# Block transposes on VectorE, 32-row score tiles and a pipeline two batches deep in a longformer-and-mixer kernel

## The chip, the cores and the metric

The kernel runs on one core of one Trainium2 chip. The metric is the device time of one execution in microseconds (us), lower is better. The profiled span, from the first to the last instruction, is 1.7 to 2.0 us shorter than the time of the same run. Positions in time below are us from the start of that span.

## The reference

The input is `q`, `k`, `v` of shape 8 x 8 x 576 x 64 (batch, head, position, depth) and eight sorted `global_idx`. A banded attention with eight global positions feeds an MLP-mixer block:

```python
scores = scale * q @ k.T                                   # per batch and head, 576 x 576
mask = (abs(i - j) <= 32) | is_global[i] | is_global[j]
attn = softmax(where(mask, scores, -1e9))
x = (attn @ v) with heads side by side                     # 8 x 576 x 512
u = x + transpose(relu(x.T @ w_tok1) @ w_tok2)             # w_tok1: 576 x 256
out = u + relu(u @ w_ch1) @ w_ch2                          # w_ch1: 512 x 1536, float32 out
```

(Shortened from numpy; the normalisation of the softmax is as usual.)

## The kernel before

Each batch is a run of units. The names are those that the profile shows:

- `T` turns q and k of a head pair from rows by position into columns (tile `pT`). `S_` makes the banded scores of a pair (`s`), with eight columns for the global queries, then `exp` (`e_all`), the band mask, and `eg`, the weights of the global queries.
- `GK` (`gk`) makes the scores of every query against the eight global keys. `OG` (`og`) sums the outputs of the global queries over all keys: the global sums.
- `PV` (`pv`) is the banded attention output, normalised into `x`. `M1` (`a1p`) and `M2` (`hp`) mix tokens, `M3` (`pu`) transposes, and `M4` (`b1p`) and `M5` (`op`) mix channels. An odd batch carries the last 64 positions of two batches as an extra tail.

```python
def cast(b, t=None):            # cut
    nc.scalar.copy(out=s["qn"][:, sl], in_=n32[0][:, sl])
    nc.vector.tensor_copy(out=s["kn"][:, sl], in_=n32[1][:, sl])
    nc.gpsimd.tensor_copy(out=vsh[b % 2][:, sl, :, 0:D], in_=n32[2][:, sl])

def T(b, p):
    pT = pss([P, 2, 8 * P], F16, name=f"pT_{b}_{p}")
    for ti, n in enumerate(("qn", "kn")):
        for t in range(NT):
            nc.tensor.transpose(out=pT[:, ti, P * t : P * t + P],
                                in_=s[n][:, t, 2 * p : 2 * p + 2, :], identity=ident)
    # ... GpSimd: global columns of qT, zero margin of kT; VectorE: two copies out of PSUM

def S_(b, p):                   # cut: score(ps, off, c) is, for the two heads of the pair,
    nc.tensor.matmul(ps[:, par, off : off + n], lhsT=kT[r, P * c : P * c + P],
                     rhs=qf[r, lo : lo + n], start=True, stop=True)   # r: 64 rows
    # ... ScalarE: exp into e_all; VectorE: mask; GpSimd: eg

def OG(b):
    for c in range(NT):
        for hf in range(2):
            nc.tensor.matmul(ps[:, hf, 0 : 4 * VW], lhsT=eg[:, c],
                rhs=vsh[b % 2][:, c, 4 * hf : 4 * hf + 4, :], start=(c == 0), stop=(c == NT - 1))
    # ... VectorE: the wanted blocks into rf, plus vg (the gathered v rows)

# the main loop: all attention and token mixing of batch b+1 between the M4 and M5 of batch b
for b in range(B):
    if b + 1 < B:
        cast(b + 1)
        globals_(b + 1)
    if b + 2 < B:
        load(b + 2)
    merge(sparse(b + 1) if b + 1 < B else [], dense(b))
```

The order of the emitted instructions is a hint only: a scheduler may reorder them on each engine.

The softmax here doesn't subtract the row's maximum and nothing guards it: scores larger than these inputs give would overflow.

Of the kernel before, what the change touches and what calls it, by code (L numbers as in the profile page):

```python
# [14 lines left out]

P = 128
# [6 lines left out]


def merge(sparse, dense):

    ts, td = sum(c for c, _ in sparse) or 1.0, sum(c for c, _ in dense) or 1.0
    i = j = 0
    a = d = 0.0
    while i < len(sparse) or j < len(dense):  # L30
        if j >= len(dense) or (i < len(sparse) and a / ts <= d / td):
            a += sparse[i][0]
            sparse[i][1]()
            i += 1
        else:
            d += dense[j][0]
            dense[j][1]()
            j += 1
# [3 lines left out]
def kernel(  # L42
# [18 lines left out]
    NP = H // 2  # L61
    NJ = DCH // P
    assert S == 576 and D == 64 and DM == 512 and DTOK == 256 and DCH == 1536
    LAST = S - P * (NT - 1)

    const = ctx.enter_context(tc.tile_pool(name="const", bufs=1))
    ab = ctx.enter_context(tc.tile_pool(name="ab", bufs=2))
    pb = ctx.enter_context(tc.tile_pool(name="pb", bufs=6))
# [15 lines left out]


    n32 = [const.tile([P, NT, H, D], F32, name=f"n32_{n}") for n in "qkv"]
    nc.gpsimd.memset(n32[0][LAST:P, NT - 1], 0.0)
    nc.gpsimd.memset(n32[1][LAST:P, NT - 1], 0.0)
    nc.gpsimd.memset(n32[2][0:WIN, 0], 0.0)
    nc.gpsimd.memset(n32[2][P - WIN : P, NT - 1], 0.0)  # L90

    def load(b):
        for ti, ten in enumerate((q, k)):
            for t in range(NT):
                n = P if t < NT - 1 else LAST
                nc.sync.dma_start(
                    out=n32[ti][0:n, t], in_=ten[b, :, P * t : P * t + n, :].rearrange("h p d -> p h d")
                )
        for c in range(NT):
            r0 = WIN if c == 0 else 0  # L100
            r1 = P - WIN if c == NT - 1 else P
            j0 = P * c - WIN + r0
            nc.sync.dma_start(
                out=n32[2][r0:r1, c], in_=v[b, :, j0 : j0 + (r1 - r0), :].rearrange("h p d -> p h d")
            )

    load(0)


    gt32 = global_idx.tensor.bitcast(I32)  # L110
    gidx_b = const.tile([P, NG], I32)
    nc.scalar.dma_start(out=gidx_b, in_=bass.AP(tensor=gt32, offset=0, ap=[[0, P], [2, NG]]))
    gidx_f = const.tile([P, NG], F32)
    nc.vector.tensor_copy(out=gidx_f, in_=gidx_b)

    ident = const.tile([P, P], F16)
    make_identity(nc, ident)
    pi_i = const.tile([P, 1], I32)
    nc.gpsimd.iota(pi_i, pattern=[[1, 1]], base=0, channel_multiplier=1)

    def int_op(name, in_, s, op):
        t = const.tile([P, 1], I32, name=name)
        nc.vector.tensor_scalar(out=t, in0=in_, scalar1=s, scalar2=None, op0=op)
        return t

    def to_f(name, in_):
        t = const.tile([P, 1], F32, name=name)
        nc.vector.tensor_copy(out=t, in_=in_)
        return t

    pf = to_f("pf", pi_i)
    p8 = to_f("p8", int_op("p8i", pi_i, 3, ALU.logical_shift_right))
    p16 = to_f("p16", int_op("p16i", pi_i, 4, ALU.logical_shift_right))
    pm8 = to_f("pm8", int_op("pm8i", pi_i, 7, ALU.bitwise_and))
    pm16 = to_f("pm16", int_op("pm16i", pi_i, 15, ALU.bitwise_and))

    it_i = const.tile([P, NT * P], I32)
    nc.gpsimd.iota(it_i, pattern=[[1, NT * P]], base=0, channel_multiplier=0)
    it_f = const.tile([P, NT * P], F32)
    nc.vector.tensor_copy(out=it_f, in_=it_i)  # L140


    oh = const.tile([P, NG], F32)
    gpp = const.tile([P, 1], F32)
    nc.vector.tensor_scalar(out=oh, in0=it_f[:, 0:NG], scalar1=pm8, scalar2=None, op0=ALU.is_equal)
    nc.vector.tensor_mul(out=oh, in0=oh, in1=gidx_f)
    nc.vector.reduce_sum(out=gpp, in_=oh, axis=AX.X)


    idx_i = const.tile([P, 4 + B], I32)  # L150
    base2 = const.tile([P, 1], F32)
    nc.vector.tensor_scalar(out=base2, in0=p8, scalar1=float(2 * S), scalar2=gpp, op0=ALU.mult, op1=ALU.add)
    for t in range(2):
        for par in range(2):
            nc.vector.tensor_scalar(
                out=idx_i[:, 2 * t + par : 2 * t + par + 1], in0=base2,
                scalar1=float((32 * t + par) * S), scalar2=None, op0=ALU.add,
            )
    basev = const.tile([P, 1], F32)
    nc.vector.tensor_scalar(out=basev, in0=p16, scalar1=float(S), scalar2=gpp, op0=ALU.mult, op1=ALU.add)  # L160
    for b in range(B):
        nc.vector.tensor_scalar(
            out=idx_i[:, 4 + b : 5 + b], in0=basev, scalar1=float(b * H * S), scalar2=None, op0=ALU.add
        )


    d1 = const.tile([P, H], F32)
    d2 = const.tile([P, H], F32)
    lo8 = const.tile([P, 1], F32)
    hi8 = const.tile([P, 1], F32)  # L170
    nc.vector.tensor_scalar(out=lo8, in0=pm16, scalar1=7.5, scalar2=None, op0=ALU.is_lt)
    nc.vector.tensor_scalar(out=hi8, in0=pm16, scalar1=7.5, scalar2=None, op0=ALU.is_gt)
    nc.vector.tensor_scalar(out=d1, in0=it_f[:, 0:H], scalar1=p16, scalar2=lo8, op0=ALU.is_equal, op1=ALU.mult)
    nc.vector.tensor_scalar(out=d2, in0=it_f[:, 0:H], scalar1=p16, scalar2=hi8, op0=ALU.is_equal, op1=ALU.mult)


    mf = const.tile([P, NT * P], F16)
    onm = const.tile([P, NT * P], F16)
    nc.vector.tensor_scalar(out=mf, in0=it_f, scalar1=gpp, scalar2=lo8, op0=ALU.is_equal, op1=ALU.mult)
    nc.vector.tensor_scalar(out=onm, in0=it_f, scalar1=float(S) - 0.5, scalar2=hi8, op0=ALU.is_lt, op1=ALU.mult)  # L180
    nc.vector.tensor_add(out=mf, in0=mf, in1=onm)


    colng = const.tile([P, NT * P], F16)
    colt = const.tile([P, NT * P], F16)
    nc.vector.tensor_scalar(out=colng, in0=it_f, scalar1=float(S) - 0.5, scalar2=None, op0=ALU.is_lt)
    for g in range(NG):
        nc.vector.tensor_scalar(out=colt, in0=it_f, scalar1=gidx_f[:, g : g + 1], scalar2=None, op0=ALU.not_equal)
        nc.vector.tensor_mul(out=colng, in0=colng, in1=colt)
    bandm = const.tile([P, NT, EW - 64], F16)  # L190
    nc.gpsimd.memset(bandm, 1.0)
    rowok = const.tile([P, NT], F32)
    dk = const.tile([P, NG], F32)
    for c in range(NT):
        nc.vector.tensor_scalar(
            out=dk, in0=gidx_f, scalar1=pf, scalar2=float(-(P * c - WIN)), op0=ALU.subtract, op1=ALU.add
        )
        nc.vector.tensor_mul(out=dk, in0=dk, in1=dk)
        nc.vector.tensor_scalar(out=dk, in0=dk, scalar1=0.5, scalar2=None, op0=ALU.is_gt)
        rk = rowok[:, c : c + 1]  # L200
        nc.vector.tensor_reduce(out=rk, in_=dk, axis=AX.X, op=ALU.min)
        if c == 0:
            nc.vector.memset(rowok[0:WIN, 0:1], 0.0)
        if c == NT - 1:
            nc.vector.memset(rowok[P - WIN : P, c : c + 1], 0.0)

        left, right = bandm[:, c, 0:64], bandm[:, c, 72:200]
        nc.gpsimd.affine_select(out=left, in_=left, compare_op=ALU.is_ge, fill=0.0, base=0, pattern=[[1, 64]], channel_multiplier=-1)
        nc.gpsimd.affine_select(out=right, in_=right, compare_op=ALU.is_ge, fill=0.0, base=64, pattern=[[1, P]], channel_multiplier=-1)
        nc.gpsimd.affine_select(out=right, in_=right, compare_op=ALU.is_ge, fill=0.0, base=0, pattern=[[-1, P]], channel_multiplier=1)  # L210
        nc.vector.tensor_scalar_mul(out=bandm[:, c, :], in0=bandm[:, c, :], scalar1=rk)
        if c > 0:
            nc.vector.tensor_mul(out=left, in0=left, in1=colng[:, P * c - 64 : P * c])
        else:
            nc.vector.memset(left, 0.0)
        nc.vector.tensor_mul(out=right, in0=right, in1=colng[:, P * c : P * c + P])


    e_all = const.tile([P, H, NT, EW], F16)
    nc.vector.memset(e_all, 0.0)  # L220
    eg = const.tile([P, NT, H, 16], F16)
    nc.gpsimd.memset(eg, 0.0)
    kgz = [const.tile([P, NP, 32], F16, name=f"kgz{i}") for i in range(2)]
# [59 lines left out]


    st = [dict() for _ in range(B)]

    def cast(b, t=None):
        s = st[b]
        if "qn" not in s:
# [259 lines left out]
    for t in range(NT):  # L549
        cast(0, t)  # L550
# [43 lines left out]
```

## Time and profile before

| | before |
|---|---|
| median of 3 runs (range) | 426.28 us (424.61 to 428.53) |
| profiled span | 422.7 us |
| first `M4` matmul of batch 0 | 94.7 us |
| first `M4` to first `M4`, batches 0 to 6 | 43.0, 45.4, 40.4, 45.4, 40.4, 43.8, 38.4 us |
| from the first `M4` of batch 7 to the end | 31.2 us |

The last three rows come from the timeline of TensorE: find the first matmul into `b1p` of each batch and subtract. Their sum is the span, which makes a ledger in which any change must show up.

From the page of the kernel before, the busy times and four rows of the 40 slices (each digit is the busy share of a slice of 10.6 us, in tenths; PEclk is the granted TensorE clock in tenths):

```profile
...
PE 331.2 (78%) x2756; PEld 179.0 (42%) x2756; DVE 212.5 (50%) x434; ACT 150.0 (35%) x273; POOL 94.2 (22%) x197
...
PE   0120242678799979997999799979998999899995
...
POOL 9578842020410032003120311031201000100000
PEclk9999999999699999999999999999999999999999
...
```

TensorE's digit is at most 2 in each of the first five slices, while that of GpSimd (POOL) is 5 to 9. From the tenth slice to the last but one it runs at 70 to 99%, and about every fourth slice is at 7 or 8.

The view of chosen stretches gives, for each, its length, the busy time of each engine with the number of instructions, the clock, the share of the DMA engines and GB/s:

```profile
...
core 0: us, PE busy (x) PEld busy (x) DVE busy (x) ACT busy (x) POOL busy (x), PEclk, DMA share, GB/s
0.00:50.00 50.00, 5.23 (x28) 2.27 (x30) 25.39 (x111) 6.69 (x7) 39.86 (x78) 1.00 1.02 164
...
183.00:201.00 18.00, 14.60 (x129) 7.27 (x127) 10.90 (x19) 14.63 (x28) 4.24 (x14) 1.00 0.49 90
201.00:223.70 22.70, 22.70 (x195) 12.77 (x194) 12.80 (x22) 2.81 (x4) 3.36 (x2) 1.00 0.60 133
...
183.10:268.90 85.80, 79.22 (x691) 43.22 (x689) 47.32 (x83) 36.49 (x67) 15.44 (x32) 1.00 0.53 111
...
```

There are two sorts of steady stretch. In 201 to 223.7 us TensorE is busy the whole time. In 183 to 201 us it works 14.60 of 18.00 us, and ScalarE, with 14.63 us, is just as loaded. The last line is a pair of batches, an even and an odd one: TensorE is busy 79.22 of 85.80 us, so 6.6 us of a pair are idle, or 3.3 us per batch.

The list of TensorE's waits up to the first `M4` (who waited, for whom, us in total, times, longest):

```profile
...
PE s_0_0_405 L336 <- POOL kT_0_383 L321: 16.1, 1, 16.1
PE og_528 L382 <- POOL eg L358: 10.9, 1, 10.9
...
```

The first score matmul waits 16.1 us for a small GpSimd memset that stands behind gathers and weight loads in GpSimd's order. The first `OG` waits 10.9 us for `eg`, on the same engine. (The largest total of the list, 16.9 us in five waits, is that of the first transposes for the cast of q, which itself waits for its load.)

TensorE's timeline at the end of a half-loaded stretch (start, duration, what, count, and the wait before it in brackets):

```profile
...
196.79 0.32 PE L369 MATMUL gk_1957<-qT_0_1781,kgz_252 128*32 128x384 f16 x1 [0.35 <-ACT e_all L345]
...
198.26 1.02 PE L492 MATMUL b1p_8_1991<-uT_1716,wc_274 128*128 128x512 f16 x4 [1.00 <-ACT b_2_1787 L495]
199.88 1.30 PE L382 MATMUL og_1976<-vsh_256,eg 128*128 128x264 f16 x10 [0.60 <-POOL eg L358]
```

Score, `exp`, mask, `eg`, `OG` is one chain inside one batch. ScalarE serves the score `exp`s and the `Relu`s of `M4` together, so TensorE waits now for `e_all`, now for `b`, now for `eg`.

### The profile page before, as it was taken

The page shows a single profiled execution, that of the slowest core. Times are in us where ns is not written, and L with a number is a line of the kernel's source. Part 1 is how long each engine was busy: PE and PEld are TensorE (multiplying, and loading weights), DVE is VectorE, ACT ScalarE, POOL GpSimd, SP SyncE. Part 2 cuts the span into 40 slices and gives each one's busy share as a digit, 9 for nine tenths or more (in the row PEclk, how much of TensorE's full clock was granted, in tenths as well). Part 3 has the DMA queues.
Part 4 walks back from the last instruction along what each step waited for, and adds up shares of the span by engine and source line. Part 5 has one row for each costly group of instructions (what it writes and reads, how often), then busy time and mean ns, then how long its engine had stood idle before and what let it go on. Part 6 is the DMA issues. An engine that isn't in the chain of part 4 may idle for free.

```text
span 422.7 us, 6930 instructions
## 1 busy us (share of the span) xinstructions
PE 331.2 (78%) x2756; PEld 179.0 (42%) x2756; DVE 212.5 (50%) x434; ACT 150.0 (35%) x273; POOL 94.2 (22%) x197
## 2 busy tenths in 40 slices
PE   0120242678799979997999799979998999899995
PEld 0000121444365437453645374536454745364452
DVE  4792070484545555466555653574555535556111
ACT  1202150218510772049106820392057203810520
POOL 9578842020410032003120311031201000100000
PEclk9999999999699999999999999999999999999999
DMA  1999999996927094616660847100110021001012
GB/s 25 191 207 198 205 198 215 206 189 118 187 54 173 26 170 80 163 50 124 128 161 28 140 86 186 51 0 2 51 50 3 2 76 50 2 26 50 25 47 79
DMA packets 123472, 42.48 MB, mean 101 GB/s; under 512 B 114609, under 2 KB 118577, under 8 KB 123441
## 3 DMA queue, kind: packets, MB, share of 16 engines
q1 hardware_dynamic: 112512, 28.32, 37.2%
q10 hardware_dynamic: 6288, 9.44, 6.5%
q0 software_dynamic: 4640, 4.29, 6.0%
q8 instruction: 21, 0.34, 0.3%
q14 instruction: 11, 0.08, 0.1%
HBM read 36.38 MB, written 9.44 MB: 108 GB/s over the span
## 4 chain that ended last, share of the span: by engine, by line
PE 58%; ACT 11%; DVE 11%; DMA 9%; POOL 5%; issue 4%; POOLq 0%; DVEq 0%; ACTq 0%
ACT e_all L345 4%; DVE e_all L357 3%; DMA gidx_b<-in_global_idx_dram 3%; DMA n_v<-in_v_dram 3%; ACT e_all L354 2%; ACT e_all L353 2%; DMA w_271<-in_moe_w_tok_dram 1%; DMA g_k_281<-in_k_dram,idx_i 1%; ACT e_all L352 1%; POOL eg L358 1%; DVE x_0_257 L424 1%; POOL vsh_255 L295 1%; DMA n_k<-in_k_dram 1%; PE op_4_4516 L518 1%; PE op_4_3805 L518 1%
## 5 line engine op out<-in xcount | busy, mean ns | idle before, releaser
L357 DVE TENSOR_TENSOR e_all<-e_all,bandm 128x1000 f16<-128x1000 f16 x64 | 40.8, 678 | 53.3 <-ACT e_all L354 49.9
L492 PEld LDWEIGHTS <-wc_274 128*128 128x128 f16 x384 | 34.4, 98 | 45.4 <-issue 16.2
L358 POOL COPY eg<-e_all 128x80 f16<-128x80 f16 x32 | 10.5, 327 | 81.7 <-DVE e_all L357 80.9
L412 PEld LDWEIGHTS <-e_all 128*128 128x128 f16 x320 | 24.9, 100 | 3.0 <-issue 1.7
L417 PEld LDWEIGHTS <-e_all 128*128 128x128 f16 x256 | 19.1, 101 | 1.3
L382 PEld LDWEIGHTS <-eg 128*128 128x128 f16 x80 | 8.1, 109 | 21.3 <-POOL eg L358 19.5
L295 POOL CAST vsh_256<-n_v 128x2560 f16<-128x2560 f32 x4 | 9.3, 2316 | 29.9 <-PE pv_4_1063 L412 8.6
L295 POOL CAST vsh_255<-n_v 128x512 f16<-128x512 f32 (+1 forms) x8 | 9.8, 1263 | 24.4 <-DMA n_v<-in_v_dram 9.3
L315 PE MATMUL pT_0_371<-ident,qn_322 128*128 128x128 f16 x5 | 1.4, 289 | 16.9 <-ACT qn_322 L293 16.9
L336 PE MATMUL s_0_0_405<-qT_0_382,kT_0_383 64*128 64x200 f16 x4 | 0.5, 351 | 16.1 <-POOL kT_0_383 L321 16.1
L454 PEld LDWEIGHTS <-w_273 128*128 128x128 f16 x80 | 7.8, 97 | 12.0 <-issue 3.2
L505 PEld LDWEIGHTS <-wc_274 128*128 128x128 f16 x192 | 11.1, 98 | 0.9
L382 PE MATMUL og_528<-vsh_255,eg 128*128 128x264 f16 x10 | 2.4, 425 | 10.9 <-POOL eg L358 10.9
L315 PEld LDWEIGHTS <-qn_322 128*128 128x128 f16 x20 | 1.9, 127 | 18.7 <-ACT qn_322 L293 17.7
L436 PEld LDWEIGHTS <-w_271 128*128 128x128 f16 x64 | 6.3, 99 | 7.3 <-issue 1.1
L293 ACT CAST qn_697<-n_q 128x2560 f16<-128x2560 f32 x1 | 2.3, 2324 | 18.9 <-DMA n_q<-in_q_dram 18.9
L522 DVE TENSOR_TENSOR osb_0_4465<-u_7_4235,op_0_4452 128x512 f32<-128x512 f16 x1 | 0.7, 686 | 15.1 <-PE op_0_4452 L518 15.1
L336 PEld LDWEIGHTS <-kT_0_383 64*128 64x128 f16 x10 | 0.7, 129 | 17.1 <-issue 16.1
L293 ACT CAST qn_322<-n_q 128x512 f16<-128x512 f32 x5 | 3.1, 617 | 12.7 <-DMA n_q<-in_q_dram 12.7
L315 PE MATMUL pT_0_371<-ident,kn_323 128*128 128x128 f16 x5 | 1.4, 288 | 7.4 <-DVE kn_323 L294 7.4
L518 PEld LDWEIGHTS <-b_7_4324 128*128 128x128 f16 x48 | 4.7, 98 | 5.4
L293 ACT CAST qn_1189<-n_q 128x2560 f16<-128x2560 f32 x1 | 2.3, 2325 | 12.8 <-DMA n_q<-in_q_dram 12.8
(1293 smaller groups left out, 957.5 us busy)
## 6 DMA issues: line engine op xcount, KB each, us to landing
n_q<-in_q_dram SPq DMA_DIRECT2D x32, 256.0 KB, 5.1
n_k<-in_k_dram SPq DMA_DIRECT2D x32, 256.0 KB, 5.3
n_v<-in_v_dram SPq DMA_DIRECT2D x24, 256.0 KB, 5.4
n_v<-in_v_dram SPq DMA_DIRECT2D x16, 192.0 KB, 5.0
wc_274<-in_moe_w_ch_dram POOLq DMA_DIRECT2D x3, 512.0 KB, 10.3
wc_275<-in_moe_w_ch_dram POOLq DMA_DIRECT2D x3, 512.0 KB, 17.3
n_q<-in_q_dram SPq DMA_DIRECT2D x8, 128.0 KB, 4.9
n_k<-in_k_dram SPq DMA_DIRECT2D x8, 128.0 KB, 4.8
```

The source lines that it names most:

```text
L295: nc.gpsimd.tensor_copy(out=vsh[b % 2][:, sl, :, 0:D], in_=n32[2][:, sl])
L345: nc.scalar.activation(out=e2[:, :, 1:3, 64:EW], in_=s1[:, :, 0:400].rearrange("p h (c x) -> p h c x", c=2), func=AF.Exp, scale=scale)
L353: nc.scalar.activation(out=e2[:, :, 4, 64 : 64 + QS], in_=s2[:, :, 136:272], func=AF.Exp, scale=scale)
L354: nc.scalar.activation(out=e2[:, :, 3, 64:EW], in_=s2[:, :, 272:472], func=AF.Exp, scale=scale)
L357: nc.vector.tensor_mul(out=eh, in0=eh, in1=bandm)
L358: nc.gpsimd.tensor_copy(out=eg[:, :, 2 * p : 2 * p + 2, 0:NG], in_=e2[:, :, :, P:QS].rearrange("p h c x -> p c h x"))
L382: nc.tensor.matmul(ps[:, hf, 0 : 4 * VW], lhsT=eg[:, c], rhs=vsh[b % 2][:, c, 4 * hf : 4 * hf + 4, :], start=(c == 0), stop=(c == NT - 1),)
L412: nc.tensor.matmul(o, lhsT=e_all[:, h, tau, QS - sh : QS - sh + P], rhs=vsh[b % 2][:, tau, h, :], start=False, stop=last and tau == NT - 1,)
L417: nc.tensor.matmul(o, lhsT=e_all[:, h, tau + 1, 0:P], rhs=vsh[b % 2][:, tau + 1, h, :], start=False, stop=last)
L492: nc.tensor.matmul(ps, lhsT=wc1[:, cc, P * j : P * j + P], rhs=s["uT"][:, cc, :], start=(cc == 0), stop=(cc == 3))
L505: nc.tensor.matmul(ps[:, i, :], lhsT=wc1[:, cc, P * j : P * j + P], rhs=s["uTl"][:, cc, :], start=(cc == 0), stop=(cc == 3),)
L518: nc.tensor.matmul(ps, lhsT=w, rhs=wc2[:, j, :], start=(j == 0), stop=(j == NJ - 1))
```

## The change

The intent is to take work off TensorE and ScalarE in the steady state and to shorten the prologue.

- q and k are loaded as float16 by casting DMAs (only batch 0's q is still cast on ScalarE), with positions spread so that VectorE can turn them: a 32 x 32 block transpose on pairs of float16 seen as one int32. TensorE's 40 transposes per batch, the two casts and the PSUM copies go.
- A pair of depth elements now shares an int32, so a score needs two accumulating matmuls with 32 rows in place of one with 64. Four heads stand in the four row groups. `GK` is tiled by rows and columns.
- `OG` is tiled by columns: four groups of 32 columns, two heads each, with half the streamed width. One-hot rows in `eg` let it pick the global v rows as well, which makes the eight v gathers unnecessary.
- The schedule is the program order on every engine. One half of a batch merges `OG`, `PV` and `M1` of batch b+1 and the VectorE transposes of b+2 into `M4` of b. The other half merges `M2` and `M3` of b+1 and the scores of b+2 into `M5` of b.
- A new prologue gathers for batches 0 to 3 only before use, and finishes the scores of batch 1 before the dense work of batch 0 begins.

```diff
+    ctx.enter_context(tc.manual_schedule(engines=ORDERED))          # ORDERED = None
...
-        for ti, n in enumerate(("qn", "kn")):
-            for t in range(NT):
-                nc.tensor.transpose(
...
+    def Xk(b, hg):
+        nc.vector.transpose(
+            out=kTs[b % 2][:, hg, WIN : WIN + S].rearrange("p (i r) -> p r i", r=RK),
+            in_=st[b]["k16"].bitcast(I32)[:, hg].rearrange("p (r j) -> p r j", r=RK),
+        )
...
+            for e in range(2):
+                for r in range(4):
+                    rs = slice(32 * r, 32 * r + 32)
+                    nc.tensor.matmul(
+                        tiles[r // 2][:, r % 2, off : off + n], lhsT=kT[rs, P * c : P * c + P, e],
+                        rhs=qf[rs, lo : lo + n, e], start=(e == 0), stop=(e == 1),
+                    )
...
+            for r in range(4):                                       # OG
                 nc.tensor.matmul(
-                    ps[:, hf, 0 : 4 * VW], lhsT=eg[:, c],
-                    rhs=vsh[b % 2][:, c, 4 * hf : 4 * hf + 4, :], start=(c == 0), stop=(c == NT - 1),
+                    ps[32 * r : 32 * r + 32, 0, 0 : 2 * VW].rearrange("p (g x) -> p g x", g=2), lhsT=egs[b % 2][:, c, r],
+                    rhs=vsh[b % 2][:, c, r::4, :], start=(c == 0), stop=(c == NT - 1),
                 )
...
+    globals_k(0)                                                     # prologue, cut
+    flush()
+    vcast(0)
+    # (two memsets) load_v(1), load_k(1, 1), load_q(1, 1)
+    u_S(0, 1, 0)()
+    u_S(0, 1, 1)()
+    u_GK(0, psv)()
+    flush()
+    # (wc1 and wc2 loads, OG and PV and M1 of batch 0, transposes of batch 1)
+    sp = phase_m(0)
+    for i, (_, f) in enumerate(phase_s(1)):
+        if i < len(sp):
+            run(sp[i][1])
+        run(f)
+    flush()
+    vcast(1)
+    gather(gq, q, 1)                                                 # gathers of batches 4 to 7
+    gather(gk, k, 1)
+    gather_t(gq, gqT, 1)
+    gather_t(gk, gkT, 1)
+    load_qk(2)
+    load_v(2)
+    for b in range(B):
...
+            ss = phase_s(b + 2)
+            Bs = Bs[:2] + ss[:1] + Bs[2:3] + ss[1:2] + Bs[3:4] + ss[2:3] + Bs[4:] + ss[3:]
+            A.append((0.0, lambda: vcast(b + 2)))
...
+        merge(A, D4)
+        merge(Bs, D5)
```

(`flush` emits what was held back, here the band mask on VectorE and `eg` on GpSimd. Lines of "..." are cuts; comments are added.)

## The prediction

> **What bounds it now.** Three stretches, read from the chain of waits (first M4 matmul of each batch): a prologue to 94.7 us, seven batches to 391.7 us (mean 42.4), and a last dense batch of 31 us. Runs read 3.6 us above the 422.7 us span.
>
> - Prologue: the table of windows has TensorE 5.2 us busy in the first 50. The index load lands at 13.1 us; twelve gathers and ten weight loads hold GpSimd to 45 us; list of waits: the first score matmul waits 16.1 us for a GpSimd memset of kT. OG then waits 10.9 us: batch 1's v cast, waiting for its load, precedes `eg` on GpSimd.
> - Steady state: TensorE. In 201-223.7 us it is busy 22.7 of 22.7 us. In 183-201 us it is busy 14.6 of 18: ScalarE (14.6 busy) serves score exps, Relus and the q cast together; exp, mask, `eg`, OG is one chain.
>
> Start-to-start times in the timeline, TensorE per batch: M4 and M5 20.7, odd-batch tails 2.7 (mean), M1+M2 4.3, M3 0.9, PV 3.3, transposes 2.2, scores 1.9, OG 1.1-1.3, GK 0.4: about 37.6. So about 5 us of each 42.4 is waiting.
>
> **Removed, added, moved, per batch.**
> - TensorE: minus 40 transposes, -2.2. OG becomes 20 column-tiled matmuls, four at once, about -0.6. GK becomes 32 matmuls in 8 rounds, about +0.6. Scores become 80 matmuls with 32 rows, four at once. Streaming is the same, weight loads double; PV's spacing shows about 30 ns each, so about +0.5. Net -1.7: about 36. [...] the trace agrees for columns (four GK matmuls start within 20 ns), none shows four row tiles.
> - VectorE: minus k cast (1.5) and eight PSUM copies (3.2 spaced), plus six block transposes. [...] x16's 512 elements take 0.69 us in the trace, so about 3 us for 2304 (estimate). Not critical.
> - ScalarE: minus q cast (2.3). GpSimd: kT memsets, vg products go; casting q/k loads come.
> - Schedule: PV, M1 and M4 in one half; M2, M3, M5 and the next-but-one batch's scores in the other. ScalarE then has about 8 us in each half of about 18, and scores no longer gate the same batch's PV. I expect the 5 us of waiting to fall to about 2: 38 per batch.
>
> **Critical path.** Six full batches x 38 = 228, one without scores 34.5, the last dense 31. Prologue: gathers shrink from twelve to four before use, masks shrink, no GpSimd inversion; but wc1 is issued after batch 0's second `eg`, and 11 MB at the observed ~200 GB/s or more must land first. Batch 0 dense starts at about 49 (40-60), with batch 1's scores already done. Total 49+228+34.5+31+3.6 = 346.
>
> **Prediction: 346 us, 326 to 366 (8 in 10). Faster by over 2%: 0.97; within: 0.02; slower: 0.01.**
>
> **Signs.** First M4 matmul at 40-60 us; batch period 36-40 us; no score-to-OG wait over 1 us; VectorE transposes 0.3-0.8 us each; ScalarE under 60% busy in either half.
>
> **What would make it wrong.** Row tiles not overlapping[...]; score tiles taking both shared PSUM buffers at once, stalling M2/M3 in order (+2 per batch); prologue loads serial behind GpSimd (+10). Upside: no waiting, about 325.

That four score tiles run at once was an assumption (the 20 ns are of columns alone); it is measured below. The 3 us for the transposes rest on the 0.69 us of `x16` alone, an estimate.

## The result

The changed kernel takes 364.95 us (median of 4 runs, 364.27 to 367.43), against 426.26 us (4 runs) of the kernel before on the same chip. Its ratio is 0.8577 (95% interval 0.8520 to 0.8634). Here and below a ratio is the mean time of one kernel's fast runs over that of the other's of the same rounds, so it is not quite the ratio of the medians quoted. All ratios in this document are to the kernel before.

| us | before | predicted | after |
|---|---|---|---|
| first `M4` of batch 0 | 94.7 | 49 | 67.2 |
| first batch | 43.0 | 38 | 43.3 |
| batches 1 to 5 | 215.4 | 190 | 191.1 |
| batch 6 | 38.4 | 34.5 | 29.6 |
| last dense batch | 31.2 | 31 | 31.2 |
| span | 422.7 | 342.5 | 362.4 |

The prediction adds 3.6 us to the span to get the time of a run. That figure compared the median of the kernel before with the span of a faster run; the profiled run of the change was 364.27 us, 1.9 above its own span.

The middle of the ledger came out almost as predicted. The first batch's excess is 5 us, batch 6 is 5 us better, and the prologue is 18 us worse. Now the profile, first the busy times and two of the rows of the page (a slice is 9.1 us here):

```profile
...
PE 307.7 (85%) x3026; PEld 161.4 (45%) x3026; DVE 185.7 (51%) x350; ACT 139.5 (38%) x264; POOL 101.9 (28%) x205
...
PE   0051956389998999999989999999899999999994
...
PEclk9997695679999999999999999999999999999998
...
```

TensorE's busy time fell by only 23.5 us, but its slices from the ninth on are at 80 to 99% up to the last. PEclk shows what the kernel before had in one slice only: in five of the slices 4 to 9 the granted clock is 5 to 7 tenths.

The view of stretches, chosen for the change: the two halves of one steady batch are the lines before the last, and the last line is a pair of batches.

```profile
...
core 0: us, PE busy (x) PEld busy (x) DVE busy (x) ACT busy (x) POOL busy (x), PEclk, DMA share, GB/s
...
46.30:62.70 16.40, 10.93 (x138) 5.32 (x137) 10.22 (x17) 7.73 (x17) 0.32 (x1) 0.70 0.69 116
67.20:75.60 8.40, 3.39 (x27) 1.86 (x24) 1.15 (x4) 0.60 (x1) 7.48 (x11) 0.50 1.02 149
225.90:242.00 16.10, 16.10 (x145) 8.88 (x142) 9.09 (x20) 7.59 (x14) 9.13 (x17) 1.00 1.05 164
242.00:262.00 20.00, 18.60 (x211) 8.63 (x211) 12.55 (x19) 8.48 (x18) 1.19 (x4) 1.00 0.11 40
...
225.90:301.60 75.70, 73.85 (x761) 38.53 (x758) 43.07 (x76) 33.93 (x65) 14.13 (x30) 1.00 0.30 64
...
```

In the steady halves TensorE is busy 16.10 of 16.10 and 18.60 of 20.00 us, and ScalarE 7.59 and 8.48: its load is now even and under half. In the pair TensorE is idle for 1.85 us, against 6.6 (3.3 us per batch) before. In 67.2 to 75.6, right after dense work begins, TensorE works 3.39 of 8.40 us at a clock of 0.50.

TensorE's waits in the first 80 us:

```profile
...
PE psc L262 <- DVE ohg L260: 17.4, 1, 17.4
PE og L404 <- POOL eg L379: 7.6, 1, 7.6
PE pv L424 <- DVE rf L410: 5.6, 2, 5.0
PE og L404 <- POOL vsh L212: 3.4, 5, 2.1
...
```

The wait for the memset is gone and scores begin at 17.4 us. The largest of the waits that follow are 7.6 us of `OG` of batch 0 for `eg`, 3.4 us of `OG` of batch 1 for the v cast, and 5.0 us of the first `PV` inside the main loop for `rf`.

For the first two, the chain that ended last shows who holds whom (start, us, what), from GpSimd's casts of v for batch 0 to those for batch 1:

```profile
...
27.47 4.62 POOL vsh L212 x5
...
34.28 1.79 POOL q L102 x3
...
36.11 0.33 POOL eg L379
...
36.48 0.77 PE og L404 x20
...
49.09 1.04 PE hp L473 x4
...
50.15 1.23 DVE u L478
...
51.42 0.61 PE s L350 x22
...
56.52 0.84 ACT e_all L359
...
61.15 2.45 DVE e_all L376 x4
...
64.11 2.84 POOL vsh L212 x5
...
```

On GpSimd the v casts, two memsets and load issues all stand ahead of `eg` at 36.11, and `OG` goes at 36.48. From 46 to 63 us `M2` and `M3` of batch 0 and the scores of batch 1 hand the chain back and forth between TensorE, ScalarE and VectorE, with no dense work to fill in: the table of stretches has TensorE at 10.93 of 16.40 us there.

For the third, the timeline of VectorE around 74 us:

```profile
...
72.60 0.24 DVE L182 STREAM_TRANSPOSE gqT<-gq 128x64 int32<-128x64 int32 x1 [8.63 <-DMA gq<-in_q_dram,idx_i]
73.52 0.24 DVE L182 STREAM_TRANSPOSE gkT<-gk 128x64 int32<-128x64 int32 x1 [0.67 <-DMA gk<-in_k_dram,idx_i]
73.69 0.73 DVE L410 TENSOR_TENSOR rf<-og,dsel 128x264 f16<-128x264 f32 x2
```

VectorE runs in program order. Two tiny transposes of gathered rows, needed for batch 4 at the earliest, stand ahead of `rf`, and the first waits 8.63 us for its gather. So the first `PV` of the main loop, which needs `rf`, starts only at 74.13 us, after 5.01 us of waiting.

Steady-state costs, from the timeline of TensorE in one `M5` half (a group's true cost is the start of the next line minus its own):

```profile
...
246.98 0.62 PE L350 MATMUL s<-qT,kT 32*128 32x200 f16 x16
247.53 0.82 PE L537 MATMUL op<-wc,b 128*128 128x512 f16 x3
...
257.19 1.47 PE L537 MATMUL op<-wc,b 128*128 128x512 f16 x6
258.58 1.25 PE L391 MATMUL gk<-qT,kg 32*32 32x512 f16 x32
259.77 0.82 PE L537 MATMUL op<-wc,b 128*128 128x512 f16 x3
261.50 0.47 PE L404 MATMUL og<-vsh,eg 128*32 128x132 f16 x20 [0.91 <-POOL eg L379]
...
```

Sixteen score matmuls of 200 columns take 0.55 us (246.98 to 247.53). `GK` takes 1.19 us. `OG` takes about 0.4 us, against 1.13 to 1.3 before. The score tiles of the four row groups do overlap here: six `M5` matmuls of 512 columns take 1.39 us (257.19 to 258.58), so sixteen times 200 columns, one after the other at that rate, would take 1.45 us (estimate), and they took 0.55.

VectorE's groups by shape (busy us, mean ns):

```profile
...
L231 DVE STREAM_TRANSPOSE kT<-k 128x576 int32<-128x576 int32 x16 | 19.9, 1244 | 4.5 <-DMA k<-in_k_dram 4.5
...
L241 DVE STREAM_TRANSPOSE qT<-q 128x320 int32<-128x320 int32 x16 | 8.0, 498 | 4.3 <-ACT q L244 4.3
L241 DVE STREAM_TRANSPOSE qT<-q 128x256 int32<-128x256 int32 x16 | 6.4, 400 | 0.0
...
```

### The profile page after: what moved, and what is told of

The parts are those of the page before. It is cut to its first block, busy times and chain, and to the rows that moved or that the text cites. A ratio compares the mean times of both kernels' runs of the same rounds, so it can differ in the third digit from the quotient of the medians.

```text
span 362.4 us, 7307 instructions
## 1 busy us (share of the span) xinstructions
PE 307.7 (85%) x3026; PEld 161.4 (45%) x3026; DVE 185.7 (51%) x350; ACT 139.5 (38%) x264; POOL 101.9 (28%) x205
## 4 chain that ended last, share of the span: by engine, by line
PE 71%; DVE 8%; ACT 7%; POOL 5%; DMA 4%; issue 3%; POOLq 0%; DVEq 0%; ACTq 0%
PE b1p L511 23%; PE op L537 20%; PE hp L473 5%; DVE e_all L376 5%; PE a1p L457 5%; PE s L350 5%; DMA v<-in_q_dram 4%; PE pv L432 3%; PE b1lp L524 3%; PE pv L424 3%; ACT e_all L359 3%; PE pv L437 2%; POOL vsh L212 2%; PE pu L491 2%; ACT e_all L365 2%
## 5 line engine op out<-in xcount | busy, mean ns | idle before, releaser
L537 PE MATMUL op<-wc,b 128*128 128x512 f16 x384 | 94.7, 380 | 0.0
L511 PE MATMUL b1p<-uT,wc 128*128 128x512 f16 x384 | 92.2, 384 | 0.0
L514 ACT ACTIVATE b<-b1p 128x512 f16<-128x512 f32 x96 | 57.4, 598 | 83.8 <-PE b1p L511 83.4
L537 PEld LDWEIGHTS <-b 128*128 128x128 f16 x384 | 34.7, 98 | 39.5 <-issue 5.4
L511 PEld LDWEIGHTS <-wc 128*128 128x128 f16 x384 | 34.8, 98 | 37.1 <-issue 1.6
L359 ACT ACTIVATE e_all<-s 128x800 f16<-128x800 f32 x32 | 25.1, 834 | 45.0 <-PE s L350 45.0
L102 POOL DMA_DIRECT2D q<-in_q_dram x56 | 34.3, 635 | 13.3 <-DMA k<-in_k_dram 6.6
L432 PE MATMUL pv<-vsh,e_all 128*128 128x66 f16 x320 | 29.7, 200 | 0.0
L444 DVE TENSOR_TENSOR x<-pv,rr 128x512 f16<-128x512 f32 (+1 forms) x40 | 27.6, 691 | 1.5
L437 PE MATMUL pv<-vsh,e_all 128*128 128x66 f16 x256 | 25.3, 200 | 0.0
L212 POOL CAST vsh<-v 128x512 f16<-128x512 f32 x40 | 25.1, 679 | 0.0
L231 DVE STREAM_TRANSPOSE kT<-k 128x576 int32<-128x576 int32 x16 | 19.9, 1244 | 4.5 <-DMA k<-in_k_dram 4.5
```

The source lines that it names most:

```text
L102: (eng or nc.gpsimd).dma_start(out=(st[b]["q16"] if dst is None else dst)[32 * r : 32 * r + 32, hg], in_=q[b, 4 * hg + r].rearrange("(a i ...
L212: nc.gpsimd.tensor_copy(out=vsh[b % 2][:, c, :, 0:D], in_=n32v[b % 2][:, c])
L359: nc.scalar.activation(out=e2[:, :, 1:3, 64:EW], in_=ps[:, :, 0:400].rearrange("p h (c x) -> p h c x", c=2), func=AF.Exp, scale=scale)
L432: nc.tensor.matmul(o, lhsT=e_all[:, h, tau, QS - sh : QS - sh + P], rhs=vs[:, tau, h, :], start=False, stop=last and tau == NT - 1,)
L437: nc.tensor.matmul(o, lhsT=e_all[:, h, tau + 1, 0:P], rhs=vs[:, tau + 1, h, :], start=False, stop=last)
L511: nc.tensor.matmul(ps, lhsT=wc1[:, cc, P * j : P * j + P], rhs=s["uT"][:, cc, :], start=(cc == 0), stop=(cc == 3))
```

## The experiments

Each kernel is the changed kernel with one edit, unless it says otherwise. All twelve ran, three to five rounds each, and all were right in value. "Better" and "worse" below compare medians with the change, which ran in other rounds; the medians of the kernel before in all these rounds lie between 424.4 and 426.3 us, so 1 to 2 us of such a difference can be noise. The times of batches and of pairs come from one trace each. "Pair" is the time of an even and an odd batch in the steady state, 85.8 us before and 75.7 us after. Theory A is that TensorE in program order sets the pair, so that work given back to it comes out at its full length; its rivals have idle time swallow it. D and E disagree on whether looking two batches ahead is worth anything. H is that the scores of batch 1, done in the open, are the largest loss of the prologue. I is that ScalarE's freedom from the q cast is the rest of the waiting.

### The steady state

**pe_transposes: 40 transposes per batch back on TensorE, as idle work.** The results are thrown away.

```diff
+    def idle_T(b, u):
+        pT = pss([P, 2, 8 * P], F16, name=f"pT_{b}_{u}")
+        src = st[b]["q16"]
+        for ti in range(2):
+            for t in range(NT):
+                nc.tensor.transpose(out=pT[:, ti, P * t : P * t + P], in_=src[:, ti, t, :], identity=ident)
...      # one call after each of the first four PV units
```

> The 40 TensorE transposes per batch are put back as idle work: same shape and number, into the shared PSUM buffers, from data already there, read by nobody, for batches 2 to 7, in the half with PV and M4. Theory A (TensorE is the limit there: 16.07 of 16.07 us busy): each batch costs 40 x 0.0555 = 2.2 us more, the pair of batches goes from 75.7 to about 80.1 us, the whole from 365 to about 378. Rival B (after the change the pace is set by chains of waits, and transposes would fill gaps): pair under 77.2, whole under 369.

Measured: 385.49 us, ratio 0.9064 (0.9021 to 0.9107). The pair is 80.2 us, up 4.5, or 2.23 us per batch: just 40 x 55.5 ns, the spacing of a transpose. So work given back to TensorE costs its full length, and theory A holds for the steady state; that the removal had paid as much is inferred from this. The whole grew by more than six batches of it (20.5 us, where 13 were expected), largely because the idle transposes of batch 2 stand in order on TensorE and waited 4.7 us for q of batch 2 in the first batch. That loss is the experiment's own.

**og_full: `OG` with full columns again.**

```diff
-            for r in range(4):
-                    ps[32 * r : 32 * r + 32, 0, 0 : 2 * VW]..., lhsT=egs[b % 2][:, c, r],
-                    rhs=vsh[b % 2][:, c, r::4, :], ...
+            for hg in range(2):
+                    ps[:, hg, 0 : 4 * VW], lhsT=egs[b % 2][:, c],
+                    rhs=vsh[b % 2][:, c, 4 * hg : 4 * hg + 4, :], ...
```

> The global sums back in the full-width form (10 matmuls of 264 columns per batch instead of 20 column-tiled ones of 132), everything else as after the change. Theory A: OG's 0.41 us becomes about 1.1, so 0.7 us per batch, pair 77.1, whole about 370. Rival B: OG waits for eg anyway in part of the batches, pair within 0.4 us of 75.7, whole within 2 us of 365.

Measured: 370.55 us, ratio 0.8725 (0.8694 to 0.8755). The pair is 77.1 us, up 1.4 (0.70 per batch). The column tiles give what they save on TensorE, so A again.

**dve_twice: each VectorE transpose of the main loop done twice.**

```diff
-        fs = [lambda: Xk(b, 0), lambda: Xq(b, 0), lambda: Xk(b, 1), lambda: Xq(b, 1)]
+        twice = lambda f, hg: (f(b, hg), f(b, hg))
+        fs = [lambda: twice(Xk, 0), lambda: twice(Xq, 0), lambda: twice(Xk, 1), lambda: twice(Xq, 1)]
```

> Every VectorE block transpose of batches 2 to 7 is done twice (same source, same destination). That is 4.1 us more VectorE work per batch (2 x 1.24 + 4 x 0.40 to 0.45 us), in the half where VectorE is busy 9 of 16 us. Theory A (VectorE off the critical path): whole within 2 us of 365, pair within 0.5 us. Rival C (the transposes at twice the predicted time delay PV's normalisation and so TensorE): pair plus 2 us or more, whole plus 6 or more.

Measured: 364.84 us, ratio 0.8594 (0.8564 to 0.8624), and a pair of 75.7 us, unchanged. The transposes are off the critical path. The prediction's cost of them (about 3 us per batch) was too low, at 4.3 us measured, and it did not matter.

**one_ahead: the scores of batch b+1 in the same iteration as its `PV`, one batch ahead as before.**

```diff
-    sp = phase_m(0)
-    for i, (_, f) in enumerate(phase_s(1)):       # scores of batch 1 leave the prologue
...
+        ss1 = phase_s(b + 1) if b + 1 < B else []
...
-        merge(A, D4)
-        merge(Bs, D5)
+        merge(ss1 + A + Bs, D4 + D5)
```

> Only the place of the scores changes: the scores of batch b+1 are computed in the iteration that also needs them (one batch ahead, as before the change), before OG and PV; all operations, program order and lags stay. Batch 1's scores leave the prologue, so the first M4 should come about 10 us earlier. Theory D (looking two batches ahead is what removes the 3 us of waiting per batch): the pair of batches rises from 75.7 to 81 us or more. Rival E (lighter TensorE work plus lags in program order are enough): pair at most 77.2.

Measured: 360.42 us, ratio 0.8481 (0.8444 to 0.8519). The pair is 79.0 us, up 3.25, between the two theories' figures: looking two batches ahead is worth about 1.6 us per batch. It is worth 6.8 us in batch 6 (36.4 against 29.6), which is left with no scores. (The edit also merges everything into one stream in place of two halves, so the 1.6 us are those of both.) And yet the whole is 4.5 us faster than the change. The first `M4` comes at 53.6 us in place of 67.2, and the first batch takes 37.0 in place of 43.3. So the depth returns 16.1 us in batches 1 to 6 (200.4 against 191.1 in batches 1 to 5, and the 6.8), and the change loses 19.9 before them, where the scores of batch 1 are made with nothing beside them. Not all of the 19.9 is the scores: TensorE's list of waits for one_ahead has no wait for `rf` in the first batch, so the 5.0 us behind the gathers are part of it.

**act_cast: an idle cast of the old q cast's size on ScalarE, once per batch in the scores' half.**

```diff
+    def idle_cast():
+        nc.scalar.copy(out=cast_out, in_=cast_in)      # 128 x 2560, float32 to float16
...
-            Bs = Bs[:2] + ss[:1] + Bs[2:3] + ss[1:2] + Bs[3:4] + ...
+            Bs = Bs[:2] + ss[:1] + Bs[2:3] + ss[1:2] + [(0.0, idle_cast)] + Bs[3:4] + ...
```

> The measured pieces explain 9.05 of the 10.1 us that a pair of batches gained (transposes 4.45, OG 1.35, two ahead 3.25), while the scores and GK cost 1.8 more by their spacing, so about 2.8 us per pair are not accounted for. Theory I: they are the q cast of 2.3 us that stood among the score exps on ScalarE. Here one idle cast of the same shape is put back per batch (batches 2 to 7) in the middle of the scores, from and to tiles nobody else uses. Theory I: pair of batches 77.5 to 79 us, whole about 370 to 374. Rival J (ScalarE, busy 8.5 of 20 us in that half, has the room): pair within 0.5 us of 75.7, whole within 2 us of 365.

Measured: 373.80 us, ratio 0.8806 (0.8764 to 0.8848). The pair is 78.2 us, up 2.5, as theory I expected. The cast itself takes 2.37 us; TensorE's waits over two pairs (150 to 310 us) show where it goes, first with the cast, then in the change:

```profile
...
PE pu L496 <- ACT e_all L364: 4.9, 4, 1.7
...
```

```profile
...
PE pu L491 <- ACT e_all L359: 0.3, 2, 0.2
```

`M3`'s second tile (`pu`) shares two PSUM buffers with the scores and waits for an `exp` to free one; with the cast ahead of that `exp` on ScalarE, the wait grows from 0.3 to 4.9 us in two pairs, or 2.3 of the 2.5 us of a pair. This is the cost of such a cast in the changed kernel. In the kernel before, TensorE waited for other tiles (`b`, `e_all`, `eg`), so that the q cast cost as much there is inferred and not shown.

**auto: the changed kernel without the fixed program order.**

```diff
-    ctx.enter_context(tc.manual_schedule(engines=ORDERED))
```

> The changed kernel with the one line that holds every engine to program order taken out, so that the scheduler orders the instructions by priority. If program order with its lags is part of the steady gain: pair of batches above 77.2 us, and inversions in the prologue as before the change (first M4 above 70), whole 372 or more. If the cheaper operations and the two-ahead structure are all of it: pair within 1 us of 75.7, whole 360 to 369.

Measured: 361.87 us, ratio 0.8493 (0.8451 to 0.8535), with a pair of 75.4 us. The first of the two theories (372 us or more) fell, and the second held. The fixed order is worth nothing in the steady state, and the scheduler's order of the prologue is slightly better: the first `M4` comes later, at 70.8, but the first batch takes 36.7 us.

**before_ordered: the kernel before, with the fixed program order added.**

```diff
+    ctx.enter_context(tc.manual_schedule(engines=None))
```

> The kernel before the change held to its own program order on every engine, nothing else. Its program puts the mask multiply right behind the exps and has no lags, so each waits at the head of its queue. If lags and the new order of work are needed: slower than 426 by 2 to 10 per cent, with the weight loads still ahead of the kT memsets on GpSimd. If program order alone is worth something: under 418.

Measured: 472.58 us, ratio 1.1067 (1.1000 to 1.1134), a little beyond the 2 to 10% expected. Batches 0 to 5 take 48 to 52 us each. In the prologue a wait of 44.7 us for a gather's cast appears, but the first `M4` still comes at 95.0 us. So the order alone does not bring the gain; with the old arrangement of units it costs 46 us. Which of the units' places costs it was not tested.

### The prologue

Four reasons could make the first dense matmul late: GpSimd's order ahead of `eg` (pool_order), the gathers of batches 4 to 7 (gather_late), batch 1's scores in the open (s1_late), or loads that no order can hasten.

**gather_late: the gathers of batches 4 to 7 into batch 0's first half, their transposes into batch 1's.**

```diff
-    gather(gq, q, 1)                 # and gk, and both gather_t, out of the prologue
...
+        if b == 0:
+            A.append((0.0, lambda: (gather(gq, q, 1), gather(gk, k, 1))))
+        if b == 1:
+            A.append((0.0, lambda: (gather_t(gq, gqT, 1), gather_t(gk, gkT, 1))))
```

> The indexed gathers of the global rows of batches 4 to 7, and their two VectorE transposes, move from before the loop into iterations 0 and 1. Theory F (the 67.2 to 74.1 us hole is VectorE standing in order behind a transpose that waits for a gather GpSimd issues only at 67 to 72 us): the hole goes, the first batch (43.3 us from its first M4 to the next) falls to about 37, whole 365 to about 358. Rival G (the hole is the loads of wc1 or batch 2, which then show instead): first batch stays over 41, whole within 2 us of 365.

Measured: 361.56 us, ratio 0.8524 (0.8460 to 0.8588): 3.4 us better, not the 7 expected. The first batch is 39.8 us, not 37. The 5.0 us for `rf` are gone, and a new wait of 2.4 us of `PV` for `x` has come. VectorE's timeline shows why:

```profile
...
67.02 0.77 DVE L410 TENSOR_TENSOR rf<-og,dsel 128x264 f16<-128x264 f32 x2 [3.37 <-PE og L404]
71.72 1.26 DVE L231 STREAM_TRANSPOSE kT<-k 128x576 int32<-128x576 int32 x1 [3.92 <-DMA k<-in_k_dram]
...
76.32 0.84 DVE L241 STREAM_TRANSPOSE qT<-q 128x320 int32<-128x320 int32 x2 [2.60 <-DMA q<-in_q_dram]
...
```

The next thing in VectorE's order is the transpose of batch 2, and that waits 3.92 and 2.60 us for its loads. One blocked instruction at the head of an ordered engine was taken away, and the next took a good part of its place.

**pool_order: `eg` ahead of the memsets and the load issues of batch 1.**

```diff
     globals_k(0)
-    flush()
     vcast(0)
-    nc.gpsimd.memset(...)            # two memsets, load_v(1), load_k(1, 1), load_q(1, 1)
+    flush()
     u_S(0, 1, 0)()
     u_S(0, 1, 1)()
     u_GK(0, psv)()
     flush()
+    nc.gpsimd.memset(...)            # the same five lines here
```

> Only GpSimd's order in the prologue: the v cast of batch 0 goes ahead of its first eg copy, and the second eg copy goes ahead of the two memsets and five load issues of batch 1 (33 to 36 us). Theory F: batch 0's OG starts at about 32.5 us instead of 36.5, and what follows moves with it: first M4 about 63, whole about 361. Rival G (the first M4 is bound by wc1's landing): first M4 stays at 66 to 68, whole within 2 us of 365.

The v cast of batch 0 moves ahead of the first `eg` as well. Measured: 360.69 us, ratio 0.8484 (0.8426 to 0.8542), 4.3 us better. The first `M4` comes at 63.7 us, and `OG`'s wait is 3.3 us in place of 7.6, as expected.

**s1_late: the scores of batch 1 merged into batch 0's `M4`.** This keeps the depth of two from batch 1 on.

```diff
-    sp = phase_m(0)
-    for i, (_, f) in enumerate(phase_s(1)):
-        if i < len(sp):
-            run(sp[i][1])
-        run(f)
+    for _, f in phase_m(0):
+        run(f)
...
+            first = phase_s(1) if b == 0 else []
...
+            A = first + A
```

> Two batches ahead is kept in the loop, but batch 1's scores and GK leave the prologue and are merged with batch 0's M4 in iteration 0. Theory H (two-ahead cost its gain because batch 1's scores ran in the prologue in the open): first M4 at 53 to 56 us as in the one-ahead run (53.6), first batch about 42, steady pair 75.7 as after the change, whole about 352. Rival: the work only moves, the second batch's first M4 stays near 110 us, whole within 3 us of 365.

Measured: 353.83 us, ratio 0.8326 (0.8270 to 0.8383), 11.1 us better. The first `M4` comes at 52.8 us, the first batch takes 45.7 (about 42 was expected), and the pair stays at 75.7 us. Theory H holds: this is the largest of the three parts. The edit also hides the gathers: the wait of 5.0 us of the first batch's `PV` for `rf` is gone.

**best: gather_late, pool_order and s1_late together.** The edit is the union of the three.

> gather_late, pool_order and s1_late together. If the three are separate pieces of the prologue: first M4 at about 49 us, first batch about 41, steady pair 75.7, last two 29.7 and 31: whole about 346 to 349. If they are one and the same wait: as the best of the three, about 352.

Measured: 352.46 us, ratio 0.8288 (0.8230 to 0.8345). That is a miss: 346 to 349 was expected. The first `M4` comes at 47.7 us, but the first batch takes 52.0 us, with a wait of 6.1 us of `OG` for `eg`. GpSimd's timeline:

```profile
...
50.36 0.60 POOL L102 DMA_DIRECT2D q<-in_q_dram  x1 [2.73 <-DMA wc<-in_moe_w_ch_dram]
53.75 0.59 POOL L108 DMA_DIRECT2D k<-in_k_dram  x1 [2.78 <-DMA wc<-in_moe_w_ch_dram]
57.08 0.62 POOL L102 DMA_DIRECT2D q<-in_q_dram  x1 [2.75 <-DMA wc<-in_moe_w_ch_dram]
60.49 0.60 POOL L102 DMA_DIRECT2D q<-in_q_dram  x1 [2.79 <-DMA wc<-in_moe_w_ch_dram]
...
63.55 0.58 POOL L379 COPY eg<-e_all 128x160 f16<-128x160 f16 x2
...
```

GpSimd issues the loads of batch 2 ahead of `eg`, and four of these issues wait 2.73 to 2.79 us each for an earlier weight load to land. The weight loads are issued at about the same time as in the change (36.0 to 40.6 us, against 36.4 to 40.7); what moved up is the issue of batch 2's loads, from 71.9 to 44.8 us, so that they meet the weight loads under way. The trace also shows which load each one waits for: the one issued eight places earlier on GpSimd. That holds for all seven issues that wait for a landing from 47 to 63 us: five wait for weight loads, and those at 62.06 and 62.96 us for the k and q loads issued at 44.84 and 45.37 us. The trace of the change shows the same wait with its semaphores: the 90 issues on GpSimd carry eight semaphore numbers in turn, from the ninth on each waits for its own number, and the issues at 23.44, 39.04 and 39.96 us start 0.28 us after the landing of the load eight places earlier. So this is a wait for a semaphore of the program, which the kernel's source does not state; a limit of the hardware is not shown.

**best2: best, with the loads of batch 2 after batch 1's first `PV`, and batch 2's transposes at the end of that half.**

```diff
-    load_qk(2)
-    load_v(2)
     for b in range(B):
...
-            A = first + A
+            if b == 0:
+                og = phase_og(1)
+                load2 = [(0.0, lambda: (load_qk(2), load_v(2)))]
+                A = first + og[:2] + load2 + og[2:] + [(2.2, lambda: M1(1, pss))] + xs
```

> The run with all three prologue edits kept a new hole: OG of batch 1 waited 6.1 us for eg, because GpSimd had to issue the loads of batch 2 first, each of which waits until the load eight places earlier (wc1, wc2) has landed. Here the loads of batch 2 are issued after batch 1's eg copies, and its block transposes come at the end of that half. If that order was the hole: wait for eg under 1.5 us, first batch (52.0 us before) about 46, whole about 346 to 348. If the prologue is bound by the bytes of wc1 and wc2 instead: the wait moves to the M5 or transposes of batch 2, whole stays at 351 to 353.

Measured: 347.33 us, ratio 0.8147 (0.8114 to 0.8179), in the range expected. The ledger is 48.8, 46.5, 191.1, 29.6 and 31.2 us. It beats the change by 17.6 us (medians) and the kernel before by 79.

## Why the prediction was right or wrong

The time, 346 us with a range of 326 to 366, held the measured 364.95, with 1 us to spare at its upper end. That it held is partly luck: the prologue came out 18.2 us too late and the first batch 5.3 too long, batch 6 was 4.9 us shorter than predicted for a reason that the prediction did not have, and the step from span to run was 1.9 us in place of 3.6. Without the error in batch 6 the time would have been about 370. The terms fared differently.

**Right: the steady state.** "38 per batch" measured 37.9 (half of 75.7 us). The parts, each from its own experiment and from spacings in the trace, per batch: transposes 2.23 (2.2 predicted), `OG` 0.70 (0.6), the second batch of depth 1.6, and ScalarE's cast 1.2, less 0.7 for the longer `GK` (1.19 against 0.47 us). That is 5.0, about what a batch lost (half of 85.8 less 75.7). The experiments undo one part each, and how the parts act together was not tried, so the close sum is a check and no proof. The stretches of a whole pair give the same split directly: TensorE's busy time fell from 79.22 to 73.85 us and its idle time from 6.6 to 1.85, per batch 2.7 us of work and 2.4 of waiting. So both parts of the predicted mechanism are there, but their sizes are not those predicted: the work fell by more than 1.7, since the scores did not get dearer (2.3 us per batch against 2.5, each matmul counted from its start to that of the next, less any gap), and the waiting fell by less than 3, since only 3.3 us were idle before and not 5.

**Right: the signs in the steady state.** No wait of `OG` is over 0.91 us in steady batches. ScalarE is at 47% and 42% in the two halves. Of the feared troubles, row tiles that do not overlap did not appear: sixteen score matmuls took 0.55 us, against the 1.45 of the estimate above for one after the other, and the scores, whose operands now step by two elements, take 2.3 us per batch against 2.5, counted in the same way.

**Mis-sized: the prologue.** The step that failed is "Batch 0 dense starts at about 49 (40-60), with batch 1's scores already done". It measured 67.2 us. I had counted the loads as the limit and the scores of batch 1 as fitting in their shadow. The runs show that they do not. Removing them alone gives 52.8 us, and fixing GpSimd's order as well gives 47.7 (best) and 48.8 (best2; both have gather_late too). So 49 is the right figure for a prologue without those scores, though no run shows that the loads, the reason given for it, set it. Some 14 of the 18 us are those scores, and about 3.5 are `eg` behind load issues ("prologue loads serial behind GpSimd" was named, at 10). The two, each taken alone, add up to 17.9 of the 18.2 us. Not all of this is lost time, since the scores must run somewhere: in s1_late the first batch grew by 2.4, even with the wait for `rf` gone, and the whole gained 11.1.

**Mis-sized: the first batch.** It was counted as a full batch of 38 and took 43.3 us, because of the blocked transposes of the gathered rows (5.0 us), for which nothing in the prediction stood. With the gathers later, the rest of the gain went to a transpose waiting for batch 2's loads.

**Mis-sized the other way: batch 6.** It was "without scores 34.5" and took 29.6. I took only the scores and their kin off the mean batch. An even batch has no odd tail, which alone is 2.7 us of the mean, and without scores the waiting of the mean batch is gone too. TensorE's own work there is `M4` and `M5` 20.7, `M1` and `M2` 4.3, `M3` 1.1 and `PV` 3.3: 29.4 of the 29.6 us (the trace lacks the record of one `M4` matmul), with no wait at all.

**Wrong without effect: VectorE's transposes.** "0.3-0.8 us each" held for q (0.50 and 0.40) and not for k (1.24 us). I took the rate of another VectorE operation, the normalisation into `x16` (512 elements in 0.69 us, or 1.35 ns per element); that the transposes would keep it was my estimate. These transposes write with steps of 18 words (k) and 2 words (q), and take 2.2 and 1.6 ns per element. No run here separates the stride from other causes, and dve_twice shows that the cost does not count.

**The role of the clock.** PEclk is 0.70 in 46.3 to 62.7 us and 0.50 in 67.2 to 75.6, and the same `GK` lasts 2.21 us at 60.4 us, against 1.25 in the steady state. In the change's record of the clock, which begins at 29.0 us, it is 0.50 in three stretches of 10.2 us each, from 32.4, 52.9 and 66.6 us, and 1.00 between them and then up to 360.1 us. The first fall came in the wait of 7.59 us for `eg`. The other two came without such a wait: in the stretches at 1.00 before them, 10.2 and 3.4 us long, TensorE was busy for 6.4 and 0.85 us, and its longest wait was 1.2 and 2.1 us. What makes the clock fall is not shown. The mean clock over the run is 0.954 for the change, 0.987 for s1_late and 0.993 for one_ahead. So parts of this prologue ran at half the clock, but how much of the 18 us is the clock was not measured apart.

**Open.** Whether the weight loads would bound a prologue below 48 us (DMA moved 202 GB/s from 20 to 60 us in best2, and both kernels show about 200 in most of their early slices) was not tried. Nor was it tried why the first batch of best2 still takes 46.5 us, 10 more than a steady even one (36.1). Its trace gives the parts but not their causes: scores and `GK` of two batches take 8.5 us on TensorE against 3.5, TensorE waits 3.5 us against 0.9, and the clock is halved for 10 us of it (the mean over the batch is 0.89). Nor was it tried why, in the prologue of the change, four band masks on VectorE took 3.82 us while GpSimd cast v, against 2.44 at 61 us, and those five v casts 4.62 us, against 2.84 at 64 us; in the trace masks and casts start by turns, one of each per 1.00 us.

## What to carry to other kernels

When a change deepens a pipeline, cost the extra stage of the prologue with nothing beside it, wait by wait, and set it against what the depth returns per iteration times the iterations: here 16 us came back, and the change lost 20 before it, of which 5 were a wait behind gathers. Where engines run in program order, look for the instruction that waits longest at the head of each engine and ask who stands behind it, and expect the next blocked one to show when it is moved. A last iteration that has lost a stage should be added up from its own operations and not taken as the mean minus that stage.
